# A fused memory attention and bilinear FFN on one Trainium2 core: the quarters of M formed on VectorE straight out of PSUM, low parts on GpSimd

## The chip, the core and the metric

The kernel runs on one core of one Trainium2 chip. The metric is the device time of one execution in microseconds (us); it was measured in three runs of the kernel before, and one more execution was taken with the profiler, whose trace the prediction reads.

## What is computed

There are 8 batches with 8 heads, 576 positions and head size 64; phi has 32 memory slots. Attention goes through the slots, and its output feeds a bilinear feed-forward net. Cut to what matters:

```python
a = softmax(phi, over positions)                  # per batch and head
k_m, v_m = a^T k, a^T v                           # 32 x 64 memories per head
attn = softmax(q k_m^T / 8, over the 32 slots)
x = attn v_m                                      # 4608 tokens x 512
h = (x w1) * (x w2)                               # 4608 x 1024
out = (h w3) w_out                                # 4608 x 512, fp32
```

## The kernel before

The kernel folds matrices together so that TensorE does less. W = w3 w_out is formed once, at the start. For each batch, v_m is multiplied into w1 and w2, which gives the batch's matrix **M**; attention probabilities **P** times M give the two factors of h directly. All large products run as three float32r products of split operands: a high part (a cast, made on ScalarE) and a low part (the value less its high part), called h and l in names: mh and ml for M, ahl for P, gh and gl for the product of the factors, Wh and Wl for W.

From batch 1 on, P times M is done as a 2 by 2 block product with seven block products instead of eight (class `Sevenths`), so besides the blocks themselves P and M need four sums of blocks each; the seven blocks and sums lie in one tile of 7 slices. `sums` makes the four sums of P on GpSimd (line 364) and the parts of all seven. `memory_weights` makes a quarter of M (M0 to M3, 256 columns of each block): it multiplies v_m with the staged weights (`weights_times`, line 385) into the two PSUM banks `a` and `b`, copies both banks to a tile x on ScalarE (line 423), makes the four sums on GpSimd (line 426), casts on ScalarE (line 133) and subtracts on VectorE (line 135), first for the three blocks, then for the four sums. The tile x has one buffer, so a quarter can't be copied out before the quarter ahead of it is through.

A batch b has two stages. In the **product stage** (`ab_stage`) TensorE does the 8 groups of seven products of batch b (line 661), pair by pair; ScalarE and VectorE combine banks `a`, `b` and `o` (lines 680 to 726), and GpSimd makes gl (line 729). In the **output stage** (`out_stage`) TensorE multiplies gh, gl with W (line 765) in blocks of 128 rows, 24 matmuls each, four blocks for an even batch and five for an odd one; ScalarE copies each block out of its PSUM bank `o`, of which there are two, to `osb` (line 775), and SP stores it. Under the output stage of batch b the attention of batch b+1 and its M run as well: scores (`sc`, line 310), their softmax in two halves (`se`, `sn`, `pr`, lines 320 to 349), `ps` (the step `sums`), and M0 to M3.

Every engine works through its instructions in the order in which the program was written; a scheduler does not move them. That order comes from hand-written strings: REST is the order of one output stage (O is a quarter of an output block, six matmuls, and with the block's last quarter its copy to osb; M0, se0 and the like go one step further in their generator; W0 to W3 start the load of a quarter's weights, and phi2, rows2, q2, kv2 start loads for batch b+2). MEETS places the steps that run inside a product stage, by pair, with a "<" for a step left over from the output stage before. One quarter O always stays for the product stage, after its first two products (q1 into bank `a`, q5 into bank `o`).

```python
REST = """
W0 W1 O blocks blocks O sc0 sc1 sc0 W2 se0 se0 sc1 O O M0 W3 M0 se0 se1 se1 M0 se1 M1 sn0 sn0 sn0 pr0 M0 M0 O
M1 M0 sn1 sn1 sn1 pr1 O M1 M1 ps M2 O ps O M1 M1 M2 O phi2 rows2 ps ps M2 M2 M3 O q2 kv2 M2 M2 O M3 O M3 M3
""".split()
```

The functions that the change touches, and what calls them:

Of the kernel before, what the change touches and what calls it, by code (L numbers as in the profile page):

```python
# [8 lines left out]
F32 = mybir.dt.float32  # L9
F32R = mybir.dt.float32r  # L10
# [4 lines left out]
ALU = mybir.AluOpType  # L15
# [25 lines left out]
B15 A15 A14 less.1 A15 A15 B14 A15 B2 A13 less.1 A2 A14 A2 A14 A13 A2 A14 less.1 B13 A14 A12 A13 A13 less.1 B12 A13  # L41
A12 mem.1 A12 A12 A12 mem.1
""".split()
MEETS = {0: "<M3 top", 1: "<M3 exp", 2: "top exp", 3: "row", 4: "norm", 6: "less less", 7: "less less less"}
REST = """
W0 W1 O blocks blocks O sc0 sc1 sc0 W2 se0 se0 sc1 O O M0 W3 M0 se0 se1 se1 M0 se1 M1 sn0 sn0 sn0 pr0 M0 M0 O
M1 M0 sn1 sn1 sn1 pr1 O M1 M1 ps M2 O ps O M1 M1 M2 O phi2 rows2 ps ps M2 M2 M3 O q2 kv2 M2 M2 O M3 O M3 M3
""".split()


# [1 line left out]
def memory_attention__then__bilinear_ffn_kernel(  # L52
# [19 lines left out]
    nc = tc.nc  # L72
    P = 128
    B, NG, S = qT.shape[0], 4, 576
    D = 64
    M = 32
    NT = 2
# [8 lines left out]
    const = ctx.enter_context(tc.tile_pool(name="const", bufs=1))  # L86
# [13 lines left out]
    NQ = 4  # L100
    FQ = DF // NQ
# [9 lines left out]
    for x, where in (("h", Wh), ("l", Wl)):  # L111
        t = const.tile([P, half, DO], F32R, name=f"W{x}0")
# [12 lines left out]
    def banks_ab():  # L125

        return [psum(ps_ab, x) for x in "ab"]
# [4 lines left out]
    def split(hi, lo, src):  # L132
        nc.scalar.copy(out=hi, in_=src)  # L133
        yield
        nc.vector.tensor_tensor(out=lo, in0=src, in1=hi.bitcast(F32), op=ALU.subtract)  # L135
# [50 lines left out]
    ready = {}  # L186

    def attention(b):
# [167 lines left out]
        def sums():  # L356
            x = v["at"].rearrange("p n (t s) -> p (n t) s", t=NT)
            hi, lo = ready["P", b] = [att.tile([P, 7, HALF], F32R, name="ahl", tag="ahl", bufs=2) for _ in range(2)]
            s = att.tile([P, 4, HALF], F32, name="sums", tag="a")

            for y, i, j, op in ((0, 3, 2, ALU.add), (1, None, 0, ALU.subtract), (2, 0, 3, ALU.subtract), (3, 1, 1, ALU.subtract)):
                p = s[:, y - 1] if i is None else x[:, i]
                q = s[:, 1] if y == 3 else x[:, j]
                nc.gpsimd.tensor_tensor(out=s[:, y], in0=p, in1=q, op=op)  # L364
            yield from split(hi[:, :3], lo[:, :3], x[:, :3])
            yield
            yield from split(hi[:, 3:], lo[:, 3:], s)

        steps = {"ps": sums, "top": top, "row": row, "less": less, "exp": exp, "norm": norm, "mem": memories, "blocks": blocks}
        steps |= {f"turn{i}": lambda i=i: turn(i) for i in (0, 4)}  # L370
        for n in range(2):
# [9 lines left out]
    def weights_times(b, q, w, ps):  # L381
        for g in range(NG):
            for t in range(NT):
                d = slice((1 - t) * D, (2 - t) * D)
                nc.tensor.matmul(
                    ps[t][g * M : (g + 1) * M], lhsT=vm[b % 2][d, g], rhs=w[d, :, g], start=True, stop=True
                )
# [19 lines left out]
    staged = {}  # L407
# [9 lines left out]
    def memory_weights(b, q):  # L417
        ps = banks_ab()
        weights_times(b, q, staged[q], ps)
        yield  # L420
        x = const.tile([P, 8, FQ], F32, name="x", tag=f"w12_{NQ - 1}")
        for t in range(NT):
            nc.scalar.copy(out=x[:, 2 * t : 2 * t + 2], in_=ps[t].rearrange("p (w f) -> p w f", w=2))  # L423
        yield
        for y, i, j in ((4, 0, 1), (6, 3, 0), (5, 3, 4), (7, 2, 5)):
            nc.gpsimd.tensor_tensor(out=x[:, y], in0=x[:, i], in1=x[:, j], op=ALU.subtract)  # L426
        mh, ml = ready["M", b][q] = [new.tile([P, 7, FQ], F32R, name=f"{z}{q}") for z in ("mh", "ml")]
        yield from split(mh[:, :3], ml[:, :3], x[:, 1:4])
        yield
        yield from split(mh[:, 3:], ml[:, 3:], x[:, 4:])  # L430


    tasks, at = [], 0
# [4 lines left out]
    CW = DF  # L438
# [292 lines left out]
    def ab_stage(b, go, before, part):  # L731
# [4 lines left out]
        for p in range(NF + 2):  # L736
            for x in order:
                if x == "+":
                    for what in MEETS.get(p, "").split():
                        if what[0] == "<":  # L740
# [48 lines left out]
    new = ctx.enter_context(tc.tile_pool(name="new", bufs=1, side="right", reuse_waits="tile"))  # L789

    def goer(b):
        begun = {}

        def go(what):
            if b + 1 == B:
                return
            if what not in begun:
                if what[0] == "M":
                    begun[what] = memory_weights(b + 1, int(what[1]))
                else:  # L800
                    begun[what] = steps[b + 1][what]()
            next(begun[what], None)

        return go
# [108 lines left out]
```

## Time and profile before

| | us |
|---|---|
| median of three runs | 579.94 (577.59 to 580.29) |
| the profiled execution's own time | 579.34 |
| its span, first to last instruction | 577.6 |
| TensorE (PE) busy, 91% of the span | 528.4 |
| VectorE (DVE) busy | 374.7 |
| ScalarE (ACT) busy | 315.9 |
| GpSimd (POOL) busy | 217.7 |

The profile calls TensorE's matmuls PE and its weight loads PEld. A busy share is an average over stages with different limits, so the table alone doesn't say what a change is worth. A matmul counts as busy at either clock, so busy time also holds the price of a low clock. In rows of the trace, out<-in gives the names of the tiles, then partitions x elements, and x with a number is how many instructions a row holds.

### The profile page before, as it was taken

How to read it: one execution, taken by the hardware profiler on the slowest of the kernel's cores; microseconds unless marked ns; L12 is line 12 of the kernel's file. 1: busy time of each engine (PE TensorE's matmuls, PEld its weight loads, DVE VectorE, ACT ScalarE, POOL GpSimd, SP SyncE). 2: the span in 40 equal slices, each digit the busy share in tenths (PEclk: the TensorE clock that was granted, in tenths of full speed). 3: DMA queues.
4: the chain of work that ended last, by engine and by line, in shares of the span. 5: the costliest groups of instructions: out<-in, count | busy, mean ns of one | idle time of the engine just before them, and what ended most of it. 6: DMA issues, size and time to landing. Idle time of an engine off the chain costs nothing.

```text
span 577.6 us, 10059 instructions
## 1 busy us (share of the span) xinstructions
PE 528.4 (91%) x3879; PEld 420.2 (73%) x3879; DVE 374.7 (65%) x643; ACT 315.9 (55%) x574; POOL 217.7 (38%) x203
## 2 busy tenths in 40 slices
PE   8999999977999699978999699968999699969997
PEld 5457698656966499657967498648967498548987
DVE  4899997675758466866757366865767366865500
ACT  7998785355635365356635365446545365446501
POOL 0000000283436524383447424383437424374500
PEclk9999999995999899997999799997999799998999
DMA  8999569827064601772075502671084512600011
GB/s 343 421 416 420 211 238 362 311 76 306 11 237 172 285 28 52 259 273 110 10 272 189 231 29 81 231 309 73 11 295 185 213 28 93 220 18 37 1 37 54
DMA packets 21823, 103.28 MB, mean 179 GB/s; under 512 B 2576, under 2 KB 3728, under 8 KB 12816
## 3 DMA queue, kind: packets, MB, share of 16 engines
q1 hardware_dynamic: 21776, 102.65, 46.3%
q8 instruction: 30, 0.49, 0.3%
q14 instruction: 17, 0.14, 0.1%
HBM read 89.00 MB, written 13.64 MB: 178 GB/s over the span
## 4 chain that ended last, share of the span: by engine, by line
PE 63%; POOL 16%; DVE 11%; ACT 6%; issue 2%; DMA 1%; SPq 0%; ACTq 0%; DVEq 0%
PE o L765 17%; PE b L661 13%; POOL x L426 10%; PE o L661 8%; PE a L661 8%; POOL sums L364 6%; DVE ml L135 4%; PE a L547 3%; ACT x L423 3%; PE b L547 3%; PE x L267 3%; PE o L547 2%; DVE s_sb L341 1%; ACT mh L133 1%; DMA raw<-in_weights 1%
## 5 line engine op out<-in xcount | busy, mean ns | idle before, releaser
L426 POOL TENSOR_TENSOR x<-x 128x256 f32<-128x256 f32 x112 | 104.0, 951 | 138.1 <-ACT x L423 135.9
L729 POOL TENSOR_TENSOR gl<-u,gh 128x576 fp32r<-128x576 f32 x56 | 79.7, 1428 | 136.4 <-ACT gh L726 134.7
L765 PE MATMUL o<-W,gh 128*128 128x512 f32 (+1 forms) x296 | 102.1, 402 | 0.0
L135 DVE TENSOR_TENSOR ml<-x,mh 128x1024 fp32r<-128x1024 f32 (+1 forms) x60 | 75.6, 1270 | 34.5 <-ACT mh L133 34.5
L661 PE MATMUL b<-ahl,mh 128*128 128x288 f32 x336 | 75.6, 308 | 3.5 <-ACT b L680 3.2
L765 PE MATMUL o<-Wh,gh 128*128 128x512 f32 (+1 forms) x148 | 62.2, 420 | 16.7 <-ACT osb L775 16.7
L133 ACT CAST mh<-x 128x1024 fp32r<-128x1024 f32 (+1 forms) x60 | 56.9, 948 | 29.8 <-POOL x L426 29.3
L765 PEld LDWEIGHTS o<-W,gh 128*128 128x128 f32 x296 | 57.5, 196 | 20.2 <-issue 8.9
L661 PE MATMUL o<-ahl,mh 128*128 128x288 f32 x224 | 50.8, 308 | 22.3 <-ACT osb L775 19.5
L661 PEld LDWEIGHTS b<-ahl,mh 128*128 128x128 f32 x336 | 54.9, 192 | 8.0 <-ACT b L680 4.0
L765 PE MATMUL o<-Wh,gl 128*128 128x512 f32 (+1 forms) x148 | 59.2, 400 | 0.0
L775 ACT COPY osb<-o 128x512 f32<-128x512 f32 (+1 forms) x37 | 21.4, 579 | 68.9 <-PE o L765 68.9
L765 PE MATMUL o<-Wl,gh 128*128 128x512 f32 (+1 forms) x148 | 59.0, 399 | 0.0
L765 PE MATMUL o<-W,gl 128*128 128x512 f32 (+1 forms) x148 | 58.6, 396 | 0.0
L765 PEld LDWEIGHTS o<-Wh,gh 128*128 128x128 f32 x148 | 29.2, 197 | 35.0 <-ACT osb L775 17.9
L661 PEld LDWEIGHTS o<-ahl,mh 128*128 128x128 f32 x224 | 37.5, 196 | 23.6 <-ACT osb L775 20.2
L661 PE MATMUL b<-ahl,ml 128*128 128x288 f32 x168 | 50.4, 300 | 0.0
L661 PE MATMUL a<-ahl,mh 128*128 128x288 f32 x224 | 49.6, 304 | 0.8 <-ACT x L423 0.8
L680 ACT COPY b<-a 128x288 f32<-128x288 f32 x56 | 21.7, 388 | 39.1 <-DVE u L719 19.9
L703 DVE TENSOR_TENSOR o<-b,a_sb 128x288 f32<-128x288 f32 x56 | 25.8, 460 | 25.2 <-PE b L661 24.9
L423 ACT COPY x<-a 128x512 f32<-128x512 f32 x28 | 16.4, 587 | 46.2 <-DVE ml L135 37.1
L661 PEld LDWEIGHTS a<-ahl,mh 128*128 128x128 f32 x224 | 38.0, 197 | 1.8 <-ACT x L423 1.3
(156 smaller groups left out, 1096.3 us busy)
## 6 DMA issues: line engine op xcount, KB each, us to landing
kv<-kept SPq DMA_DIRECT2D x21, 1024.0 KB
kv<-in_kv SPq DMA_DIRECT2D x16, 1024.0 KB, 11.4
raw<-in_weights SPq DMA_DIRECT2D x10, 1024.0 KB, 18.6
q<-in_qT SPq DMA_DIRECT2D x8, 1152.0 KB
out<-osb SPq DMA_DIRECT2D x31, 256.0 KB, 2.0
q<-kept SPq DMA_DIRECT2D x7, 1024.0 KB, 5.4
raw<-in_weights SPq DMA_DIRECT2D x12, 512.0 KB, 4.1
ph<-in_phiT SPq DMA_DIRECT2D x9, 576.0 KB, 4.0
```

The source lines that it names most:

```text
L133: nc.scalar.copy(out=hi, in_=src)
L135: nc.vector.tensor_tensor(out=lo, in0=src, in1=hi.bitcast(F32), op=ALU.subtract)
L364: nc.gpsimd.tensor_tensor(out=s[:, y], in0=p, in1=q, op=op)
L423: nc.scalar.copy(out=x[:, 2 * t : 2 * t + 2], in_=ps[t].rearrange("p (w f) -> p w f", w=2))
L426: nc.gpsimd.tensor_tensor(out=x[:, y], in0=x[:, i], in1=x[:, j], op=ALU.subtract)
L547: nc.tensor.matmul(pw[r][i], lhsT=x[:, i * P : (i + 1) * P], rhs=y, start=k == 0 and j == 0, stop=k == NF - 1 and j == len(pairs) - 1,)
L661: nc.tensor.matmul(ps, lhsT=x[:, j], rhs=y[:, i], start=start and k == 0, stop=stop and k == 2, skip_group_check=True,)
L680: nc.scalar.copy(out=self.u, in_=self.a)
L703: nc.vector.tensor_tensor(out=self.c, in0=self.u, in1=self.s5, op=ALU.add)
L729: nc.gpsimd.tensor_tensor(out=self.cut(gl), in0=self.gr, in1=self.cut(gh).bitcast(F32), op=ALU.subtract)
L765: nc.tensor.matmul(ps, lhsT=x[f][:, at : at + P], rhs=y[f][:, cols], start=f == 0 and k == 0, stop=f == NF - 1 and k == 2,)
L775: nc.scalar.copy(out=osb[:, cols], in_=ps)
```

## The change

It rewrites how a quarter of M and the parts of P are made, and moves steps in the two strings.

- `memory_weights`: ScalarE copies only one block (t4, 256 columns) to x, and casts the other three straight from PSUM to mh. VectorE makes the four sums, one operand from PSUM each, in an order that builds them one on another, and subtracts the low parts of the three blocks, again out of PSUM. ScalarE then casts the four sums in one piece, and GpSimd subtracts their low parts in two pieces. A quarter has four steps instead of six.
- The tile x holds two quarters' sums, used by M0 and M3 and by M1, and M2 takes a buffer of the tile `u`, which the product stage uses for gr: three buffers in place of one.
- `sums`: GpSimd subtracts both low parts of P, which VectorE did.
- REST and MEETS: both exponentials go ahead of M0's copies, phi2 and rows2 go ahead of q2, M1's product comes one O later, M3's last steps come earlier, and inside the product stage top, exp, row, norm and less come one pair earlier.

```diff
-MEETS = {0: "<M3 top", 1: "<M3 exp", 2: "top exp", 3: "row", 4: "norm", 6: "less less", 7: "less less less"}
+MEETS = {0: "<M3 top", 1: "top exp", 2: "exp row", 3: "norm", 5: "less less", 6: "less less", 7: "less"}
 REST = """
...
+W0 W1 O blocks blocks O sc0 sc1 sc0 W2 se0 se0 sc1 se0 O se1 se1 se1 O M0 W3 phi2 rows2 sn0 sn0 sn0 pr0 M0 M0 O M1 M0 M1
+sn1 sn1 sn1 pr1 O O ps M1 M2 q2 M2 O ps M1 O M2 O M3 kv2 M3 M2 O M3 M3
...
-            yield from split(hi[:, :3], lo[:, :3], x[:, :3])
-            yield
-            yield from split(hi[:, 3:], lo[:, 3:], s)
+            for i, j, y in ((0, 3, x[:, :3]), (3, 7, s)):
+                nc.scalar.copy(out=hi[:, i:j], in_=y)
+                nc.gpsimd.tensor_tensor(out=lo[:, i:j], in0=y, in1=hi[:, i:j].bitcast(F32), op=ALU.subtract)
+                yield
...
-        yield
-        x = const.tile([P, 8, FQ], F32, name="x", tag=f"w12_{NQ - 1}")
-        for t in range(NT):
-            nc.scalar.copy(out=x[:, 2 * t : 2 * t + 2], in_=ps[t].rearrange("p (w f) -> p w f", w=2))
-        yield
-        for y, i, j in ((4, 0, 1), (6, 3, 0), (5, 3, 4), (7, 2, 5)):
-            nc.gpsimd.tensor_tensor(out=x[:, y], in0=x[:, i], in1=x[:, j], op=ALU.subtract)
+        (b12, b11), (b21, b22) = [[x[:, k * FQ : (k + 1) * FQ] for k in range(2)] for x in ps]
+        yield
+        if "x" not in staged:
+            staged["x"] = const.tile([P, 2, 4, FQ], F32, name="x", tag=f"w12_{NQ - 1}")
+        if q == 2:
+            x = const.tile([P, CW], F32, name="u", bufs=2).rearrange("p (k f) -> p k f", k=4)
+        else:
+            x = staged["x"][:, int(q == 1)]
+        t1, t2, t3, t4 = [x[:, k] for k in range(4)]
         mh, ml = ready["M", b][q] = [new.tile([P, 7, FQ], F32R, name=f"{z}{q}") for z in ("mh", "ml")]
-        yield from split(mh[:, :3], ml[:, :3], x[:, 1:4])
-        yield
-        yield from split(mh[:, 3:], ml[:, 3:], x[:, 4:])
+        firsts = ((0, 1, b11), (1, 3, ps[1].rearrange("p (k f) -> p k f", k=2)))
+        nc.scalar.copy(out=t4, in_=b12)
+        for i, j, y in firsts:
+            nc.scalar.copy(out=mh[:, i:j], in_=y)
+        yield
+        for y, p, r in ((t1, t4, b11), (t3, b22, t4), (t2, b22, t1), (t4, b21, t2)):
+            nc.vector.tensor_tensor(out=y, in0=p, in1=r, op=ALU.subtract)
+        for i, j, y in firsts:
+            nc.vector.tensor_tensor(out=ml[:, i:j], in0=y, in1=mh[:, i:j].bitcast(F32), op=ALU.subtract)
+        yield
+        nc.scalar.copy(out=mh[:, 3:], in_=x)
+        for k in range(0, 4, 2):
+            y = slice(3 + k, 5 + k)
+            nc.gpsimd.tensor_tensor(out=ml[:, y], in0=x[:, k : k + 2], in1=mh[:, y].bitcast(F32), op=ALU.subtract)
```

Two places show how the order moves. The first is ScalarE at the end of the output stage of batch 2, from the cast of P's four sums on. In it mh_2640 and mh_2692 of the kernel before are M2 and M3, mh_2578, mh_2628 and mh_2682 after the change are M1, M2 and M3, and the last osb but one is the copy of the third output block. Before:

```order
L133 CAST ahl<-sums 128x1152
L133 CAST mh_2640<-x 128x768
L133 CAST mh_2640<-x 128x1024
L423 COPY x<-a 128x512
L423 COPY x<-b 128x512
L775 COPY osb<-o 128x512
L133 CAST mh_2692<-x 128x768
L680 COPY b<-a 128x288
L684 COPY a_sb<-o 128x288
L775 COPY osb<-o 128x512
L133 CAST mh_2692<-x 128x1024
```

With the change:

```order
L366 CAST ahl<-sums 128x1152
L441 CAST mh_2578<-x 128x1024
L432 COPY x<-a 128x256
L434 CAST mh_2682<-a 128x256
L434 CAST mh_2682<-b 128x512
L441 CAST mh_2628<-u 128x1024
L441 CAST mh_2682<-x 128x1024
L789 COPY osb<-o 128x512
L694 COPY b<-a 128x288
L698 COPY a_sb<-o 128x288
L789 COPY osb<-o 128x512
```

The copy of the third block still stands behind M3; now M3's last cast is ahead of it as well, and what these casts wait for is VectorE and no longer GpSimd.

The second place is GpSimd in the same output stage, from M0 up to the first gl of the product stage. Before (line 426 are the sums of a quarter of M, line 364 those of P):

```order
L426 TENSOR_TENSOR x<-x 128x256 x8
L364 TENSOR_TENSOR sums<-at 128x288
L364 TENSOR_TENSOR sums<-sums,at 128x288
L364 TENSOR_TENSOR sums<-at 128x288
L364 TENSOR_TENSOR sums<-at,sums 128x288
L426 TENSOR_TENSOR x<-x 128x256 x8
L729 TENSOR_TENSOR gl_622<-u,gh_614 128x576
```

With the change:

```order
L444 TENSOR_TENSOR ml_2548<-x,mh_2547 128x512 x2
L364 TENSOR_TENSOR sums<-at 128x288
L364 TENSOR_TENSOR sums<-sums,at 128x288
L364 TENSOR_TENSOR sums<-at 128x288
L364 TENSOR_TENSOR sums<-at,sums 128x288
L367 TENSOR_TENSOR ahl<-at,ahl 128x864
L367 TENSOR_TENSOR ahl<-sums,ahl 128x1152
L444 TENSOR_TENSOR ml_2579<-x,mh_2578 128x512 x2
L444 TENSOR_TENSOR ml_2629<-u,mh_2628 128x512 x2
L444 TENSOR_TENSOR ml_2683<-x,mh_2682 128x512 x2
L743 TENSOR_TENSOR gl_622<-u,gh_614 128x576
```

Ahead of P's sums there is now one quarter of M instead of two; behind them come P's two low parts and then M1, M2 and M3, all of them ahead of the first gl.

## Rows read from the trace of the kernel before

**Rows 1.** What TensorE waited for: us in total, times, longest us

```profile
PE o L661 <- ACT osb L775: 19.5, 3, 6.5
PE o L765 <- ACT osb L775: 16.7, 3, 5.6
PE b L661 <- ACT b L680: 3.2, 1, 3.2
PE o L661 <- ACT ahl L133: 2.0, 1, 2.0
PE a L661 <- ACT x L423: 0.8, 1, 0.8
PE o L661 <- DVE ahl L135: 0.8, 1, 0.8
```

**Rows 2.** Stretches around seven transitions: length, PE busy, granted clock, DMA share, GB/s

```profile
128.00:141.00 13.00, 8.76 (x29) 0.50 0.97 380
196.00:200.00 4.00, 3.33 (x8) 0.57 0.42 161
261.00:268.50 7.50, 5.82 (x21) 0.54 0.37 145
322.00:330.00 8.00, 5.14 (x13) 0.57 0.46 183
387.00:398.00 11.00, 6.38 (x23) 0.53 0.51 207
452.00:460.00 8.00, 5.87 (x16) 0.57 0.38 151
517.00:524.50 7.50, 3.42 (x11) 0.54 0.09 35
```

**Rows 3.** Chain that ended last, from 236 to 264: start, us, what

```profile
239.00 0.76 DVE small L336
...
241.64 0.78 DVE at L349
...
254.06 3.20 POOL x L426 x3
...
258.67 1.05 ACT mh L133
...
262.14 0.50 ACT osb L775
...
262.68 1.09 PE o L661 x3
```

**Rows 4.** Timeline of PE and DVE, output stage of batch 2: start, us

```profile
236.13 0.61 PE L385 MATMUL a<-kv,vm 64*32 64x512 f32 x1
...
236.88 0.76 DVE L329 TENSOR_TENSOR s_sb<-s_sb,small 128x576 f32<-128x576 f32 x1
...
238.01 0.50 PE L765 MATMUL o<-Wh,gh 128*128 128x512 f32 x1
...
255.88 0.29 PE L661 MATMUL a<-ahl,ml 128*128 128x288 f32 x1
```

**Rows 5.** VectorE by line; min/median/max ns where three numbers stand

```profile
L703 DVE TENSOR_TENSOR o<-b,a_sb 128x288 f32<-128x288 f32 x56 | 25.8, 460 | 25.2 <-PE b L661 24.9
...
L341 DVE TENSOR_TENSOR s_sb<-s_sb,small x16: 745/901/1065, 58.4 to 504.0; 128x576 f32<-128x576 f32 x16
...
L338 DVE TENSOR_SCALAR small<-small x16: 174/176/415, 57.4 to 503.5; 128x18 f32<-128x18 f32 x16
```

**Rows 6.** ScalarE, a copy of 256 columns out of PSUM: busy us, mean ns

```profile
L775 ACT COPY osb<-o 128x256 f32<-128x256 f32 x2 | 0.7, 373 | 4.8 <-PE o L765 4.8
```

**Rows 7.** GpSimd by line: min/median/max ns, first and last start

```profile
L729 POOL TENSOR_TENSOR gl<-u,gh x56: 1417/1429/1440, 145.2 to 548.2; 128x576 fp32r<-128x576 f32 x56
...
L364 POOL TENSOR_TENSOR sums<-at x14: 801/1215/1627, 122.1 to 510.9; 128x288 f32<-128x288 f32 x14
```

**Rows 8.** DMA issues: a staged quarter of weights, KB, median us to landing

```profile
q<-kept SPq DMA_DIRECT2D x7, 1024.0 KB, 5.4
```

More of the change, by code (lines that the diff above doesn't have):

```diff
@@ L43 @@
 """.split()
-MEETS = {0: "<M3 top", 1: "<M3 exp", 2: "top exp", 3: "row", 4: "norm", 6: "less less", 7: "less less less"}
+MEETS = {0: "<M3 top", 1: "top exp", 2: "exp row", 3: "norm", 5: "less less", 6: "less less", 7: "less"}
 REST = """
-W0 W1 O blocks blocks O sc0 sc1 sc0 W2 se0 se0 sc1 O O M0 W3 M0 se0 se1 se1 M0 se1 M1 sn0 sn0 sn0 pr0 M0 M0 O
-M1 M0 sn1 sn1 sn1 pr1 O M1 M1 ps M2 O ps O M1 M1 M2 O phi2 rows2 ps ps M2 M2 M3 O q2 kv2 M2 M2 O M3 O M3 M3
+W0 W1 O blocks blocks O sc0 sc1 sc0 W2 se0 se0 sc1 se0 O se1 se1 se1 O M0 W3 phi2 rows2 sn0 sn0 sn0 pr0 M0 M0 O M1 M0 M1
+sn1 sn1 sn1 pr1 O O ps M1 M2 q2 M2 O ps M1 O M2 O M3 kv2 M3 M2 O M3 M3
 """.split()
@@ L419, in memory_weights @@
         weights_times(b, q, staged[q], ps)
+        (b12, b11), (b21, b22) = [[x[:, k * FQ : (k + 1) * FQ] for k in range(2)] for x in ps]
         yield
-        x = const.tile([P, 8, FQ], F32, name="x", tag=f"w12_{NQ - 1}")
-        for t in range(NT):
-            nc.scalar.copy(out=x[:, 2 * t : 2 * t + 2], in_=ps[t].rearrange("p (w f) -> p w f", w=2))
+        if "x" not in staged:
[5 more added lines that the diff above has]
+        t1, t2, t3, t4 = [x[:, k] for k in range(4)]
+        mh, ml = ready["M", b][q] = [new.tile([P, 7, FQ], F32R, name=f"{z}{q}") for z in ("mh", "ml")]
+        firsts = ((0, 1, b11), (1, 3, ps[1].rearrange("p (k f) -> p k f", k=2)))
+        nc.scalar.copy(out=t4, in_=b12)
+        for i, j, y in firsts:
+            nc.scalar.copy(out=mh[:, i:j], in_=y)
         yield
-        for y, i, j in ((4, 0, 1), (6, 3, 0), (5, 3, 4), (7, 2, 5)):
-            nc.gpsimd.tensor_tensor(out=x[:, y], in0=x[:, i], in1=x[:, j], op=ALU.subtract)
-        mh, ml = ready["M", b][q] = [new.tile([P, 7, FQ], F32R, name=f"{z}{q}") for z in ("mh", "ml")]
-        yield from split(mh[:, :3], ml[:, :3], x[:, 1:4])
+        for y, p, r in ((t1, t4, b11), (t3, b22, t4), (t2, b22, t1), (t4, b21, t2)):
+            nc.vector.tensor_tensor(out=y, in0=p, in1=r, op=ALU.subtract)
+        for i, j, y in firsts:
+            nc.vector.tensor_tensor(out=ml[:, i:j], in0=y, in1=mh[:, i:j].bitcast(F32), op=ALU.subtract)
         yield
-        yield from split(mh[:, 3:], ml[:, 3:], x[:, 4:])
+        nc.scalar.copy(out=mh[:, 3:], in_=x)
+        for k in range(0, 4, 2):
+            y = slice(3 + k, 5 + k)
+            nc.gpsimd.tensor_tensor(out=ml[:, y], in0=x[:, k : k + 2], in1=mh[:, y].bitcast(F32), op=ALU.subtract)
     tasks, at = [], 0
```

## The prediction

> **What bounds the kernel now.** I first read the waits of TensorE, since it is busy in most of the span. [rows 1] show that its idle time has almost one cause: six waits of 5.6 and 6.5 us for an osb copy on ScalarE, three in front of an output block and three in front of q5, and four smaller ones in the first transition. They add up to 19.5 + 16.7 + 3.2 + 2.0 + 0.8 + 0.8 = 43.0 us, all at the end of seven output stages. The windows around these waits come next: [rows 2] show the granted clock at 0.50 to 0.57 there, so TensorE also works at 1.2 instead of 2.4 GHz for a while after each wait; it fell after TensorE had stood still. In these seven windows it was busy for 38.7 us. The stretches at full clock in them are at most the sum of (2 x clock - 1) x length, 4.7 us, so between 34.0 and 38.7 us of work ran at half clock, which would take half as long at full clock: a loss of 17.0 to 19.4 us. I take 17.0. Everything around the transitions is dense, so TensorE is the bound and the waits are what can be won.
>
> Why it waits, the chain tells [rows 3]: GpSimd's sums for M2 end at 257.3 and the last of them at 258.7, ScalarE then casts them, VectorE makes the low part, which frees x; only then can ScalarE copy M3 out, and the osb copy at 262.14 is written behind those copies. The output block itself was ready: TensorE had worked through the next one as well and finished its last product before the wait at 256.17 [rows 4]. So the copy is held by its queue alone, and q5 starts at 262.68 because it needs that bank.
>
> **What is removed.** x is no longer one buffer and M's sums leave GpSimd, so the chain of copy, GpSimd, cast, VectorE, copy is gone in each quarter. If nothing replaced it, 43.0 + 17.0 us would go.
>
> **What is added, on one ruler.** I lay out the output stage of batch 2, from M0 at 236.13 on.
>
> TensorE: M0 and M1 together take 238.01 - 236.13 = 1.88, so 0.94 each [rows 4]. From 236.13 to 256.17 it did four of these, eleven quarters of output blocks and q1 (0.55, the last two rows of its work), so a quarter with its switching takes (20.04 - 3.76 - 0.55) / 11 = 1.43. With the change M0, a quarter, M1 and two quarters end at 242.30. Then M2 needs the banks of M0, and these are now free when VectorE's six operations on M0 are over, not when ScalarE has copied them. That is a new wait.
>
> VectorE: its last score step ends at 237.64 [rows 4]. The half softmax up to `at` took 3.42 there, from 239.00 to 242.42 [rows 3], with one instruction at 1.07 that takes 0.745 undisturbed and one at 0.42 that takes 0.176 [rows 5]; GpSimd is now idle beside it, so 2.86. The exponential it waits for now stands ahead of osb and M0 on ScalarE. So `at` is done at 240.50. The trace has no VectorE operation of 256 columns with one operand in PSUM, but 288 take 0.460 [rows 5] and 576 with both in SBUF 0.76 [rows 4], a slope of 1.04 ns a column: 0.43 for 256, 0.69 for 512. M0's six are 5 x 0.43 + 0.69 = 2.84 and end at 243.34. TensorE waits **1.04 us** in front of M2. M2 and three quarters then end at 248.57. VectorE's second half softmax runs beside GpSimd's low parts of M0 and takes 3.02, M1's six 2.84: 249.20. TensorE waits **0.63 us** in front of M3, which ends at 250.14; five quarters and q1 end at 257.84, where q5 comes.
>
> The Trainium skill ("VectorE: DVE Perf Modes", section Rules for kernel authors) advises for elementwise work on a matmul's output either to accept the plain rate from PSUM or to copy to SBUF first where many operations follow, which speaks against this edit with its six. If reading PSUM cost half the rate, the six would take 4.7 us and the two waits would grow by 3.7 us a stage, 26 us in all, to 559. The rows just used show the same slope from either memory, so the sum goes without it.
>
> GpSimd: M0's sums are done at 242.22, ScalarE's cast of 1024 columns (1.05, [rows 3]) at 243.27. From 288 columns in 0.80 and 576 in 1.43 [rows 7] a column costs 2.2 ns: the two pieces of M0 take 2.6, P's four sums 3.2, its low parts of 864 and 1152 columns 2.06 and 2.69. With `at` ready at 246.36, P is complete at 254.3, 3.5 us ahead of q5. The bound from above is P's sums at 1.63 [rows 7], when VectorE works beside them, and it becomes a rival below. The work that VectorE does beside P's parts reads one operand from PSUM, and gl never took over 1.44 us [rows 7] beside such operations; I take the lower value.
>
> ScalarE: P's second cast ends at about 250.8, M1's at 251.8, M3's copies (0.37 + 0.37 + 0.59, [rows 6] and the osb copy) at 253.1, M2's cast at 254.2; VectorE's sums of M3 follow the copy and end at 254.9, so M3's cast ends at 255.9 and the osb copy behind it at 256.5, 1.3 us ahead of q5. Where the next thing is late, it is this copy. In odd stages there are four quarters more in front of q5, and the copies are further ahead.
>
> SP and the loads: the store of the first block moves behind both exponentials, to about 239, and W3 queues behind it; 1024 KB take 5.4 us to land [rows 8], so 245, and M3 needs it at 249.2. phi2 and rows2 go behind W3. The moves inside the product stage keep three pairs between row and less. I cost all this at nothing; the cover is 4 us.
>
> The first transition has three quarters fewer in front of q5: on this ruler TensorE is there at 253.55, P's low part at 254.3 and ScalarE's copy of bank a about 0.6 behind TensorE's need, 1.35 us more.
>
> **Sum**, against the profiled execution's own 579.34: - 43.0 - 17.0 + 7 x (1.04 + 0.63) + 1.35 + 0.7 (an extra switch of 0.1 a stage) = **533 us**. That execution lies 0.6 below the median of the runs, which changes nothing. The new waits are a fifth of the old ones in length and come after long full work, so I expect the clock to stay full.
>
> **Rivals.**
> 1. *VectorE holds the banks longer.* The six operations lie on one another, and an operation disturbed by GpSimd went from 0.745 to 1.065 [rows 5], a factor of 1.43. At that price they take 4.06; the waits become 2.26 and 1.84, 2.43 us a stage more: 550. For it: nothing hides them now. Against: no row with a PSUM operand is stretched. 14%.
> 2. *The old queue stays.* The osb copy still stands behind M3. If VectorE or ScalarE is 3 us later there than laid out, q5 of the even stages waits 2 us, and the clock may fall again: 533 + 3 x 2 + up to 3 x 2 = 545. That would be the change not doing what it says, in part. 5%.
> 3. *GpSimd becomes the bound.* With everything at the disturbed rate, M0 ends at 248.5, P's sums at 255.0 and its low parts at 264.5. Even stages then wait 6.7 us, and about 2.4 for the clock, odd ones 0.9, the first 11 and 4.4: about 45 us back, 578, no change. For it: P's low parts, 4.7 us, have moved onto the chain. 7%. The Trainium skill ("SBUF — State Buffer", section Who interferes with whom) says that a VectorE tensor_tensor contends with GpSimd's reads where both its inputs are in SBUF. By that rule the new VectorE work, with an input in PSUM, leaves GpSimd alone; the undisturbed gl agrees, and the chance stays low for it.
> 4. *Slower than before: gl queues behind M's low parts.* M1, M2 and M3 follow P on GpSimd and all stand ahead of the first gl; `u` has two buffers, so the third pair's gr waits for the first gl. It decides once M3's low parts end later than some 9 us after q1, about 266: in the layout they end at 262.2, at the disturbed rate at 280. Then every stage pays some 11 us on top of rival 3: 578 + 77 = 655. It needs all of GpSimd's work disturbed. 3%.
>
> **Chances and range.** The forecast gets 70%; its own range is 523 to 543: below, the waits in front of M2 and M3 vanish and the half-clock loss is 19.4 (517 at the extreme); above, they double. Rivals 1 and 2 reach to 550; 1% is left for anything else. Rivals 3 and 4 are left out of the range, which runs from 523 to 552 and leaves some 17% outside. A difference under 0.5%, 2.9 us, can't be told from none here. Faster by more than that: 93% (the forecast, rivals 1 and 2, the odd 1%, and the 3% of rival 3 that come out below 576); within it: 4%, the rest of rival 3; slower: 3%, rival 4.
>
> **What would show it.** Right: the waits of TensorE for osb are gone or under 1 us each; new waits of about 1 us in front of M2 and 0.6 in front of M3, for VectorE, seven of each; granted clock 1.00 through the transitions from 196 on; P's low parts on GpSimd at about 2.1 and 2.7 us; six VectorE operations of a quarter in 2.8 us; the first gl no later behind q1 than now. Wrong: a clock row at 0.5 in an even stage (rivals 2 or 3, told apart by whether ScalarE or GpSimd released q5), VectorE operations of 256 columns over 0.5 us (rival 1), VectorE waiting for gl in the product stage (rival 4).

## The result, and the profile after

The changed kernel takes **529.88 us** (median of four executions, 528.88 to 531.52) against 580.12 for the kernel before on the same chip: a ratio of 0.914, 95% interval 0.910 to 0.918. The profiled execution took 529.76, with a span of 528.0. The forecast was 533, the range 523 to 552.

The waits of TensorE in the changed kernel (us in total, times, longest us) answer to [rows 1]:

```profile
PE a L386 <- ACT mh L434: 3.5, 7, 0.5
...
PE o L675 <- POOL ahl L367: 0.9, 1, 0.9
```

No line with osb is left. What is left in the transitions is a wait in front of a quarter of M (L386), once in each, and in the first transition 0.9 for P's low part.

The stretches around three of the seven transitions, each from M0 to past q5 (length, PE busy, PEld, DVE, ACT, POOL busy, granted clock, DMA share, GB/s), answer to [rows 2]:

```profile
109.00:129.00 20.00, 18.60 (x123) 11.16 (x122) 17.64 (x37) 11.53 (x22) 11.23 (x9) 1.00 0.72 264
161.00:183.00 22.00, 21.52 (x134) 13.69 (x133) 18.60 (x38) 12.54 (x23) 13.18 (x11) 1.00 0.83 310
221.00:244.00 23.00, 22.48 (x141) 14.61 (x140) 18.81 (x39) 13.36 (x25) 13.98 (x11) 1.00 0.82 315
```

The clock is at 2.4 GHz throughout; in [rows 2] it was at 0.50 to 0.57 behind each wait.

VectorE in the output stage of batch 2, from M0's six operations to M3's (start, busy us; several at a time are merged):

```profile
225.70 0.38 DVE L437 TENSOR_TENSOR x<-x,a 128x256 f32<-128x256 f32 x1
...
227.46 0.68 DVE L439 TENSOR_TENSOR ml<-b,mh 128x512 fp32r<-128x512 f32 x1
228.06 0.74 DVE L336 TENSOR_REDUCE small<-s_sb 128x18 f32<-128x576 f32 x1
228.83 0.85 DVE L338 TENSOR_SCALAR small<-small 128x18 f32<-128x18 f32 x1
...
230.01 1.50 DVE L341 TENSOR_TENSOR s_sb<-s_sb,small 128x576 f32<-128x576 f32 x1
231.55 0.78 DVE L349 STREAM_TRANSPOSE at<-s_sb 128x576 f32<-128x576 f32 x1
...
234.01 0.68 DVE L439 TENSOR_TENSOR ml<-b,mh 128x512 fp32r<-128x512 f32 x1
```

GpSimd and TensorE in the same stage:

```profile
228.37 2.53 POOL L444 TENSOR_TENSOR ml<-x,mh 128x512 fp32r<-128x512 f32 x2 [10.30 <-ACT mh L441]
232.47 0.81 POOL L364 TENSOR_TENSOR sums<-at 128x288 f32<-128x288 f32 x1 [1.57 <-DVE at L349]
...
237.65 2.70 POOL L367 TENSOR_TENSOR ahl<-sums,ahl 128x1152 fp32r<-128x1152 f32 x1
```

```profile
227.75 0.39 PE L779 MATMUL o<-W,gh 128*128 128x512 f32 x1
...
229.30 0.50 PE L779 MATMUL o<-W,gh 128*128 128x512 f32 x1
...
233.29 0.39 PE L779 MATMUL o<-Wl,gh 128*128 128x512 f32 x1
234.19 1.01 PE L386 MATMUL a<-kv,vm 64*32 64x512 f32 x2 [0.52 <-ACT mh L434]
...
235.86 0.50 PE L779 MATMUL o<-W,gh 128*128 128x512 f32 x1
...
243.06 0.29 PE L675 MATMUL a<-ahl,ml 128*128 128x288 f32 x1
243.19 0.42 PE L675 MATMUL o<-ahl,mh 128*128 128x288 f32 x2
```

ScalarE's copy of the third block, which q5 needs:

```profile
241.15 0.58 ACT L789 COPY osb<-o 128x512 f32<-128x512 f32 x1
```

M0's six operations run from 225.70 to 228.14, 2.44 us. Then comes the second half softmax, 4.27 us from 228.06 to 232.33, with L338 at 0.85 and L341 at 1.50; both start while GpSimd works off the low parts of M0 (228.37 to 230.90). M1's six end at 234.69, so M3 on TensorE starts at 234.19 with its bank a and at 234.84 with bank b. The last product of the quarter ahead of it started at 233.29. Where nothing is waited for, M follows 0.33 behind such a product and lasts 1.02 until the next one (M0 in this stage); here the next one started at 235.86, so M3 waited 235.86 - 233.29 - 1.35 = 1.22. M2, with 227.75 and 229.30, waited 0.2. Read so, all seven stages show 0.20 to 0.21 for M2 and 1.17 to 1.22 for M3. The list names ScalarE's cast for this wait; M1's cast had long ended, and VectorE's reading of bank a ended at 234.09.

### The profile page after: what moved, and what is told of

The parts are those of the page before. It is cut to its first block, busy times and chain, and to the rows that moved or that the text cites. A ratio compares the mean times of both kernels' runs of the same rounds, so it can differ in the third digit from the quotient of the medians.

```text
span 528.0 us, 10212 instructions
## 1 busy us (share of the span) xinstructions
PE 516.9 (98%) x3879; PEld 407.2 (77%) x3879; DVE 360.9 (68%) x741; ACT 295.4 (56%) x574; POOL 205.4 (39%) x161
## 4 chain that ended last, share of the span: by engine, by line
PE 65%; DVE 22%; DMA 5%; issue 4%; ACT 2%; POOL 1%; SPq 0%; ACTq 0%; DVEq 0%
PE o L779 22%; PE b L675 13%; PE o L675 8%; PE a L675 8%; DMA kv<-in_weights 4%; DVE s_sb L341 3%; PE x L267 3%; DVE s_sb L320 2%; DVE small L327 2%; DVE s_sb L329 2%; PE a L561 2%; DVE x L437 2%; PE b L561 2%; DVE small L336 2%; DVE small L338 1%
## 5 line engine op out<-in xcount | busy, mean ns | idle before, releaser
L444 POOL TENSOR_TENSOR ml<-x,mh 128x512 fp32r<-128x512 f32 x42 | 53.5, 1295 | 120.2 <-ACT mh L441 120.2
L779 PEld LDWEIGHTS o<-W,gh 128*128 128x128 f32 x296 | 55.1, 188 | 25.1 <-issue 14.7
L675 PE MATMUL b<-ahl,mh 128*128 128x288 f32 x336 | 73.5, 301 | 0.2 <-DVE gr L725 0.2
L779 PE MATMUL o<-Wh,gh 128*128 128x512 f32 (+1 forms) x148 | 59.2, 400 | 0.0
L779 PE MATMUL o<-Wl,gh 128*128 128x512 f32 (+1 forms) x148 | 57.1, 386 | 0.0
L779 PE MATMUL o<-Wh,gl 128*128 128x512 f32 (+1 forms) x148 | 56.9, 384 | 0.0
L675 PE MATMUL b<-ahl,ml 128*128 128x288 f32 x168 | 49.6, 295 | 0.0
L675 PE MATMUL o<-ahl,mh 128*128 128x288 f32 x224 | 48.3, 296 | 0.9 <-POOL ahl L367 0.9
L733 DVE TENSOR_TENSOR u<-b,gr 128x288 f32<-128x288 f32 x56 | 25.6, 458 | 24.6 <-PE b L675 24.4
L725 DVE TENSOR_TENSOR gr<-b,a_sb 128x288 f32<-128x288 f32 x56 | 25.4, 454 | 22.8 <-PE b L675 22.1
L740 ACT CAST gh<-u 128x576 fp32r<-128x576 f32 x56 | 37.4, 679 | 1.6 <-DVE u L733 1.6
```

Of the source, the lines that this page charges most:

```text
L444: nc.gpsimd.tensor_tensor(out=ml[:, y], in0=x[:, k : k + 2], in1=mh[:, y].bitcast(F32), op=ALU.subtract)
L675: nc.tensor.matmul(ps, lhsT=x[:, j], rhs=y[:, i], start=start and k == 0, stop=stop and k == 2, skip_group_check=True,)
L725: nc.vector.tensor_tensor(out=self.c22, in0=self.u, in1=self.s5, op=ALU.add)
L733: nc.vector.tensor_tensor(out=self.gr[:, 1], in0=self.u, in1=self.c22, op=ALU.mult)
L740: nc.scalar.copy(out=self.cut(gh), in_=self.gr)
L779: nc.tensor.matmul(ps, lhsT=x[f][:, at : at + P], rhs=y[f][:, cols], start=f == 0 and k == 0, stop=f == NF - 1 and k == 2,)
```

## The experiments

Ten kernels. A time without a range is of one execution; the kernel before had medians of 579.1 to 579.7 beside them.

### Which part carries the gain

**The new order alone.** The kernel before, with the order strings of the change (each of its steps of M and P mapped, so that with one x every quarter's last step stands ahead of the next quarter's copy):

```diff
-W0 W1 O blocks blocks O sc0 sc1 sc0 W2 se0 se0 sc1 O O M0 W3 M0 se0 se1 se1 M0 se1 M1 sn0 ...
+W0 W1 O blocks blocks O sc0 sc1 sc0 W2 se0 se0 sc1 se0 O se1 se1 se1 O M0 W3 phi2 rows2 sn0 ...
```

> The kernel before with the new order alone: exponentials ahead of M0, the loads and the osb copies moved, the product stage's steps moved; sums of M still on GpSimd out of one x, low parts of P still on VectorE. Theory A (the one x buffer ties ScalarE's queue, and the osb copy in it, to GpSimd's chain of sums): the chain of four quarters is as long as before, so TensorE still waits for osb, 35 to 50 us in all, with the half clock behind the waits, and the time is 565 to 590. Theory C (the order brings the gain, since the exponentials no longer stand behind osb and M0): the osb waits fall below 15 us and the time is 545 or less.

641.86: neither. It is 62 us slower than before. The waits:

```profile
PE o L765 <- ACT osb L775: 43.7, 3, 14.6
PE o L661 <- ACT osb L775: 32.8, 3, 10.9
PE a L661 <- ACT x L423: 19.7, 4, 8.0
```

They are of the same kind as in [rows 1], and together more than twice as long (96.2 against 43.0). In batch 2 the osb copy starts 35.3 us behind M0 (254.28 to 289.62), where before it was 25.9 (236.13 to 262.02). Of these 9.4 us, 1.4 come from M0's copies, which now stand behind both exponentials, so that GpSimd's sums begin later. Another 4.3 come from the place of the osb copy itself: before, it stood right behind M3's copies, and now it stands behind M3's last cast, which waits for M3's sums:

```profile
288.67 1.04 ACT L133 CAST mh<-x 128x1024 fp32r<-128x1024 f32 x1 [2.40 <-POOL x L426]
289.62 0.58 ACT L775 COPY osb<-o 128x512 f32<-128x512 f32 x1
```

In the rest of the way P's four sums stand ahead of M1's on GpSimd; what that alone costs was not taken apart. So theory A holds for what is waited for, and its size was wrong: for the old chain the new order is the worse one.

**One x with the new engines.** The kernel after, VectorE's sums and all, with one buffer:

```diff
-        if q == 2:
-            x = const.tile([P, CW], F32, name="u", bufs=2).rearrange("p (k f) -> p k f", k=4)
-        else:
-            x = staged["x"][:, int(q == 1)]
+        x = staged["x"][:, 0]
```

> The kernel after with all quarters in one x buffer and the steps of M1, M2 and M3 put so that each quarter's last step stands ahead of the next quarter's copy; VectorE's sums out of PSUM and P's low parts on GpSimd stay. Theory A: M2's copy on ScalarE has to wait for M1's low parts, which stand behind P's low parts on GpSimd (242.9 on the clock of batch 2, M0 at 221.5), M3's copy for M2's low parts (249.4), M3's cast ends at 253.5 and osb behind it at 254, 11 us behind TensorE's need at 243.2: osb waits of 11 us in even stages, 5 us in odd ones, with half clock behind them: 530 + 3 x 11 + 4 x 5 + about 20 = 590 to 605. Theory B (VectorE's faster sums bring the gain, buffers only a little): waits under 2 us a stage, 530 to 545.

612.86. The waits:

```profile
PE o L779 <- ACT osb L789: 26.2, 3, 8.8
PE o L675 <- ACT osb L789: 19.5, 3, 6.6
PE a L675 <- DVE ml L439: 15.2, 4, 6.7
```

Theory A, a little above its 590 to 605. M2's copy stands idle on ScalarE until GpSimd has done M1's low parts:

```profile
266.92 0.37 ACT L432 COPY x<-a 128x256 f32<-128x256 f32 x1 [5.05 <-POOL ml L444]
```

**Two x buffers.** The same lines, with two in turn and no use of `u`:

```diff
+        x = staged["x"][:, q % 2]
```

> The kernel after with two x buffers in turn (M0 and M2 in one, M1 and M3 in the other) and nothing else changed. Theory A: only M3's copy is held, by M1's low parts behind P's on GpSimd (242.9 on the clock of batch 2); M3's sums end at 246, its cast at 247, osb at 247.6, 4.4 us behind TensorE's need at 243.2 in the even stages, in time in the odd ones, which have four quarters (5.7 us) more in front of q5: 530 + 3 x 4.4 + up to 3 x 4 for the clock = 543 to 556, waits for osb in three stages alone. Theory B: as after, 530 within 3.

564.8, where theory A allowed up to 556. The waits are 10.8 and 7.9 for osb and 4.4 in the first transition; they come in all six later transitions and not in three, since osb is needed by an output block too (2.6 us each) where q5 is far. The third buffer is worth 35 us, of which 10.8 + 7.9 + 4.4 = 23.1 are waits. The other 11.8 are put down to the lower clock behind them: its mean is 0.978 here and 1.00 in the kernel after, which can cost up to 0.022 x 563 = 12.4.

**The old order with the new code.** The order strings of before, on the kernel after (M0's six ahead of the softmax, M2 and M3 with two quarters between them):

```diff
-... se0 O se1 se1 se1 O M0 W3 phi2 rows2 sn0 sn0 sn0 pr0 M0 M0 O M1 ...
+... O O M0 W3 M0 se0 se1 se1 M0 se1 M1 sn0 sn0 sn0 pr0 M0 O M1 ...
```

> The kernel after with the order strings of before (M's and P's steps mapped onto their new, fewer steps): M0's six operations ahead of the softmax on VectorE, the exponentials behind M0's copies, the loads for the next batch late again, top, exp and row in their old places in the product stage. Theory A (the buffers and VectorE's sums carry the gain, the new order little): 526 to 536. Theory C (the new order is needed for it, because the exponentials behind M0's copies make P late): P's low parts release q5 in even stages, waits of 3 us or more there, 540 or more.

556.53 (554.58 to 558.56), ratio to before 0.961 (0.957 to 0.964). The number is theory C's, the mechanism is not: P does not release q5. TensorE waits in front of M3:

```profile
PE a L386 <- ACT ahl L366: 18.8, 6, 3.1
PE a L386 <- DVE ml L439: 2.7, 1, 2.7
```

```profile
241.63 0.42 DVE L439 TENSOR_TENSOR ml<-a,mh 128x256 fp32r<-128x256 f32 x1
...
242.15 1.03 PE L386 MATMUL a<-kv,vm 64*32 64x512 f32 x1 [3.13 <-ACT ahl L366]
```

```profile
242.00:246.00 4.00, 3.85 (x19) 1.56 (x20) 0.64 (x2) 2.37 (x3) 4.00 (x5) 0.50 0.00 0
246.00:248.00 2.00, 2.00 (x6) 1.52 (x6) 1.14 (x3) 1.25 (x4) 2.00 (x1) 0.50 0.86 254
248.00:250.00 2.00, 2.00 (x10) 1.63 (x9) 1.39 (x4) 1.47 (x3) 2.00 (x3) 0.89 1.04 385
```

M3 needs the banks of M1, and M1's six stand behind both half softmaxes on VectorE; VectorE's last reading of bank a (L439) ends at 242.05, 0.1 ahead of M3. The old order gives TensorE too little other work until then. The windows show what a wait of 3.13 costs on top: the clock stands at half for some 6 us behind it.

**The buffers with the old engines.** ScalarE's raw copies go into two buffers in turn, GpSimd's sums into two more, and all low parts of M and P are on VectorE, each step as early as the buffers let it.

```diff
+        r = staged["x"][:, q % 2]
+        x = const.tile([P, CW], F32, name="u", bufs=2).rearrange("p (k f) -> p k f", k=4)
...
-            nc.vector.tensor_tensor(out=y, in0=p, in1=r, op=ALU.subtract)
+            nc.gpsimd.tensor_tensor(out=y, in0=p, in1=s, op=ALU.subtract)
```

> The buffers without the change of engines: ScalarE's raw copies into two buffers in turn, GpSimd's sums into two more, all low parts of M and of P on VectorE, as in the kernel before; the new order with each quarter's steps as early as the buffers let them. GpSimd has four quarters at 3.0 to 4.0 and P's sums at 3.2 to 6.4 one behind the other, from 226.5 on the clock of batch 2: M3's sums end at 242 to 249, its cast 1 later, osb behind it at 243.7 to 250.7, where TensorE needs it at 242. Theory A (what counts is that the copies no longer wait for GpSimd's chain): 1.7 to 5 us in three stages with half clock behind the longer ones, 530 to 550. Theory B (the sums must leave GpSimd): waits for osb as before or nearly, in six stages, 560 to 580.

593.54 (592.92 to 595.23), ratio 1.025 (1.022 to 1.028): slower than before, beyond theory B. GpSimd works without a gap for long, and its operations stand beside VectorE's low parts. P's sums, which take 0.80 in the kernel after:

```profile
250.88 1.70 POOL L364 TENSOR_TENSOR sums<-at 128x288 f32<-128x288 f32 x1 [0.29 <-DVE at L349]
252.65 1.51 POOL L364 TENSOR_TENSOR sums<-sums,at 128x288 f32<-128x288 f32 x1
```

M3's sums end 27.6 behind M0's start here (239.56 to 267.19). That is not later than before, where it was 29.1 (236.13 to 265.24). But the osb copy stands behind M3's last cast in the new order, and so it starts 28.6 behind M0, where before it was 25.9:

```profile
267.23 1.04 ACT L437 CAST mh<-u 128x1024 fp32r<-128x1024 f32 x1 [2.92 <-POOL u L434]
268.18 0.58 ACT L785 COPY osb<-o 128x512 f32<-128x512 f32 x1
```

By these numbers it is that place of the copy that makes this kernel slower than before. It is not shown by a run: the same buffers with the copy left ahead of M3's casts were not tried.

Buffers, engines and order are not three shares of a sum. Against the whole change, the two others without the order lose 27 us, without the engines 64, without the buffers 83, and the order alone 112.

### VectorE's sums out of PSUM or out of a raw copy

**Sums on VectorE out of a raw copy.** Three result buffers, VectorE's sums and GpSimd's work as in the change, but with ScalarE's raw copy in between:

```diff
+        for t in range(NT):
+            nc.scalar.copy(out=r[:, 2 * t : 2 * t + 2], in_=ps[t].rearrange("p (w f) -> p w f", w=2))
...
-        for y, p, r in ((t1, t4, b11), (t3, b22, t4), (t2, b22, t1), (t4, b21, t2)):
+        for y, p, s in ((t1, b12, b11), (t3, b22, b12), (t2, b22, t1), (t4, b21, t2)):
```

> The kernel after, but ScalarE first copies each quarter out of PSUM into one raw buffer, as the kernel before did and as the Trainium skill advises where many operations follow (VectorE: DVE Perf Modes, Rules for kernel authors), and VectorE's sums and first low part read SBUF alone; results in x, u, u, x; order and GpSimd's work as in the change. Theory D (VectorE's reading of the banks makes the waits in front of M2 and M3): ScalarE's copy frees them at about 226.5 and 229 on the clock of batch 2, so both waits go, 7 x 1.5 = 10 us, against it P's sums on GpSimd, which now stand beside VectorE operations with both operands in SBUF: at 1.6 instead of 0.8 each, as where that happened in the kernel before, P is complete at 243.5, where TensorE needs it at 241.7: 1.8 us back in even stages, 3 in the first: 529.9 - 10 + 3 x 1.8 + 3 = 528, within 523 to 534. If GpSimd is not touched: 520. Rival (the copies through SBUF cost more than they free, since M2's raw copy waits in ScalarE's queue for VectorE's six on M1, and osb behind it): 535 to 545.

589.31 (587.79 to 591.41), ratio 1.018 (1.014 to 1.022). All three numbers of the expectation were far too low. Theory D had the waits right: read as above, nothing is waited for in front of M2 and M3 in any stage. What it had mis-sized is what came back. VectorE on M0 and M3 of one stage, and GpSimd beside M3:

```profile
242.37 1.51 DVE L437 TENSOR_TENSOR x<-x 128x256 f32<-128x256 f32 x4
243.80 0.95 DVE L438 TENSOR_TENSOR ml<-x,mh 128x768 fp32r<-128x768 f32 x1
...
258.80 6.07 DVE L437 TENSOR_TENSOR x<-x 128x256 f32<-128x256 f32 x4 [1.00 <-ACT x L433]
264.79 2.02 DVE L438 TENSOR_TENSOR ml<-x,mh 128x768 fp32r<-128x768 f32 x1
```

```profile
260.29 5.71 POOL L443 TENSOR_TENSOR ml<-u,mh 128x512 fp32r<-128x512 f32 x4
266.02 3.17 POOL L443 TENSOR_TENSOR ml<-x,mh 128x512 fp32r<-128x512 f32 x2
```

On M0, with GpSimd idle, the work takes 2.38 us, as much as out of PSUM (2.44). On M3, beside GpSimd's low parts, the same work takes 8.01, and GpSimd's pieces go from 1.29 to 1.43 and 1.58 each. M1 to M3 together take 16.1 instead of 7.6, and waits for the one raw buffer add 0.78 + 1.00. P's sums on GpSimd, expected at 1.6 each, took 0.83 to 1.00: VectorE paid the larger part. M3's cast and the osb copy behind it come that much later, and the osb waits are back (24.8 + 15.2). Two raw buffers were not tried, so a part of the loss belongs to the single one.

The prediction set the Trainium skill's advice for a matmul's output, to accept the plain rate from PSUM or to copy to SBUF first where many operations follow ("VectorE: DVE Perf Modes", section Rules for kernel authors), against the slopes in [rows 4, 5]. The run decides: the copy fails here, and not because of the reading rate (2.38 against 2.44).

The Trainium skill ("SBUF — State Buffer", section Who interferes with whom) says that a VectorE operation with two inputs in SBUF contends with a GpSimd operation that reads SBUF, and that one with at most one input there doesn't, outside the modes in which VectorE uses both of its ports. The sums and low parts of this run and of the kernel after agree: 256 columns out of SBUF alone took 0.38 us with GpSimd idle and up to 1.83 beside it, and with one operand in PSUM never more than 0.43. L338 has one input, in SBUF, and was held all the same (0.85 instead of 0.18), so it could only fall under that exception; no run here shows the mode it ran in.

### What TensorE still waits for

**The low parts out of PSUM done twice**, 1.09 us more of VectorE in each quarter:

```diff
-        for i, j, y in firsts:
+        for i, j, y in firsts * 2:
             nc.vector.tensor_tensor(out=ml[:, i:j], in0=y, in1=mh[:, i:j].bitcast(F32), op=ALU.subtract)
```

> The kernel after with the two low parts out of PSUM on VectorE done twice, 0.41 + 0.68 = 1.09 us more in each quarter. Theory D (VectorE's six operations hold M0's and M1's banks, so the prediction's waits are theirs): M2's wait grows from 0.25 to 1.35, M3's from 1.25 by 2.18 - 1.10 to 2.33, 7 x 2.18 = 15 us: 543 to 549, and the list of waits names VectorE's ml in front of M2 or M3. Theory E (ScalarE's casts release M3, as the list names them): VectorE has that much slack, 529 to 533.

539.02, 9.1 us more: theory D's direction, theory E is out, and the size is below D's 13 to 19. The list names ScalarE's copies in front of M2 and M3 and not VectorE's ml, as D had expected. Read in the way shown above, M2 waits 1.13 in batch 2 (1.35 expected) and M3 1.72 (2.33 expected). For M3 a part fell away: the second half softmax had moved against GpSimd's pieces, so that only L338 met one, and it took 3.85 instead of 4.27:

```profile
231.64 1.16 DVE L338 TENSOR_SCALAR small<-small 128x18 f32<-128x18 f32 x1
...
233.14 0.76 DVE L341 TENSOR_TENSOR s_sb<-s_sb,small 128x576 f32<-128x576 f32 x1
```

**M0's low parts behind P's sums** on GpSimd, by a step boundary behind P's sums:

```diff
-... pr0 M0 M0 O M1 M0 M1 sn1 sn1 sn1 pr1 O O ps M1 M2 ...
+... pr0 M0 M0 O M1 M1 sn1 sn1 sn1 pr1 O O ps M0 ps M1 M2 ...
```

> The kernel after with one thing moved: the low parts of M0 on GpSimd stand behind P's sums, no longer beside VectorE's second half softmax; VectorE's and TensorE's order stay as in the change. Theory D (GpSimd's pieces beside it stretch that half softmax from 2.77, as it took in the run with the softmax first, to 4.27): it takes 2.8, M1's six end 1.4 earlier and the wait in front of M3 (1.25) goes; M2's 0.25 stays. P is complete later by M0's low parts less the 1.4, some 1.2 us, which leaves 0.4 us ahead of q5 in even stages and adds some 2.4 in the first transition: 529.9 - 7 x 1.25 + 2.4 = 523.5, within 521.5 to 526. Theory E (the stretch is VectorE's own, not GpSimd's): L338 and L341 stay at 0.85 and 1.50 there, M3's wait stays: 530 to 535.

526.36 (524.63 to 528.57), ratio 0.907 (0.905 to 0.910). Of theory D the mechanism is shown. All sixteen L338 and L341 (min/median/max ns) are undisturbed, and TensorE's wait in front of M3 is gone:

```profile
L338 DVE TENSOR_SCALAR small<-small x16: 176/177/177, 56.7 to 458.9; 128x18 f32<-128x18 f32 x16
...
L341 DVE TENSOR_TENSOR s_sb<-s_sb,small x16: 745/759/759, 57.6 to 459.4; 128x576 f32<-128x576 f32 x16
```

The median is just above what was expected, and the first transition is where it goes: it waits for P's low parts 1.1 and 1.9, where 0.9 stood. These 2.1 us more are less than the 2.4 that were expected, but the clock stands at half behind them, which the expectation had not counted:

```profile
132.00:134.00 2.00, 2.00 (x7) 1.61 (x7) 0.00 (x0) 0.40 (x1) 2.00 (x3) 0.50 0.99 418
```

From M0 of this transition to M0 of the next it is 55.77 us instead of 51.98. The profiled execution, 528.57, is the slowest of the four; its first M0 already starts 2.3 later than in the kernel after (111.57 against 109.30).

**Both half softmaxes first.** VectorE does them ahead of M0's six, P's sums stand ahead of M0's low parts on GpSimd, and two quarters of output blocks move to the place between M1 and M2.

```diff
-... pr0 M0 M0 O M1 M0 M1 sn1 sn1 sn1 pr1 O O ps M1 M2 q2 M2 O ps M1 O M2 O M3 ...
+... pr0 M0 O M1 M1 sn1 sn1 sn1 pr1 M0 O O ps M0 ps M1 O O M2 q2 M2 ps M1 O M3 ...
```

> The kernel after with both halves of the softmax ahead of M0's six operations on VectorE, P's sums ahead of M0's low parts on GpSimd, and two quarters of output blocks moved from between M2 and M3 to between M1 and M2. Theory D (TensorE's waits in front of M2 and M3, 0.25 and 1.25 us, come from VectorE, whose second half softmax was stretched from 2.9 to 4.27 us by GpSimd's low parts of M0 beside it): with GpSimd idle beside both halves they take 2.9 each, at is complete 4 us earlier, M0's six end at 230.3 on the clock of batch 2 and M1's at 232.8, where TensorE is at 230.5 and 232.9: the waits go, 7 x 1.5 to 1.8 us: 517 to 521, ratio to after 0.977 to 0.983. Theory E (those 1.5 us are switching and issue of TensorE, or ScalarE's casts as the list of waits names them): no change, 528 to 531; the wait in front of M3, named for ScalarE, stays at 0.5.

**521.45** (520.58 to 521.60), ratio to before 0.899 (0.897 to 0.901): 8.4 us less than the change, and the fastest of all. The second half softmax takes 2.77 us (223.23 to 226.00), no wait for a quarter of M is listed (read as above, the 1.2 in front of M3 is gone in all stages and 0.24 in front of M2 is left), and from M0's start to the end of q1 it is 20.66 (219.02 to 239.68) instead of 21.86. 7 x 1.20 = 8.4, the whole gain. The 1.5 to 1.8 a stage that theory D expected counted in M2's wait, which stayed: the time is 0.4 above its range.

**P's low parts on VectorE again**, the first behind M1's six and the second behind M2's:

```diff
-                nc.gpsimd.tensor_tensor(out=lo[:, i:j], in0=y, in1=hi[:, i:j].bitcast(F32), op=ALU.subtract)
+                nc.vector.tensor_tensor(out=lo[:, i:j], in0=y, in1=hi[:, i:j].bitcast(F32), op=ALU.subtract)
```

> The kernel after with P's low parts on VectorE again, the first behind M1's six operations, the second behind M2's. Theory F (moving them to GpSimd took about 2.5 us off VectorE's path to M3's cast and the osb copy behind it): M2's six end at 238.5 on the clock of batch 2, the second low part at 240.2, M3's six at 242.7, the cast at 243.7 and osb at 244.3, 1.1 us behind TensorE's need: waits for osb of about 1 us in three stages, 531 to 537. Theory G (their place is indifferent, since VectorE and GpSimd both have room): 528 to 531. If VectorE's operations are stretched by GpSimd beside them, up to 545.

537.83 (537.45 to 537.97), ratio 0.928 (0.927 to 0.930): theory F, 0.8 above its range. The waits for osb are the expected 1.1 in three stages; 3.0 in the first transition, where 0.9 stood, had not been counted. With 0.6 in front of output blocks they make 6.1 of the 8.0; the rest has no row of its own:

```profile
PE o L675 <- ACT osb L789: 3.4, 3, 1.2
PE a L675 <- DVE ml L439: 2.1, 1, 2.1
...
PE b L675 <- ACT b L694: 0.9, 1, 0.9
```

So moving P's low parts is worth 8 us, although GpSimd takes 4.7 us for what costs VectorE 2.6.

## Why the prediction came out right

**The waits: right.** All of 43.0 us [rows 1] went. The osb copy ends at 241.73 in batch 2, 1.46 ahead of q5 (1.3 was laid out). The experiments with one and two x buffers show the chain named in the prediction: ScalarE's copies held by x, and osb in their queue.

**The clock: right, undersized.** The loss of 17.0 was taken from bounds of 17.0 to 19.4. By the result, 579.34 - 529.76 = 49.6 less 43.0, plus what came back (7 x 1.82 + 0.9), leaves 20.2. The term's own working shows where the rest was lost: in [rows 2] all of the low clock was caught (the windows' lengths times 1 - clock add up to 27.2, the span times 1 - 0.953 to 27.1), so the choice of the lower bound, which took every stretch at full clock for work, was the mistake. The upper bound, 19.4, would have given 530.7. The 0.8 beyond it stays open. The 1.82 is not the reason: all three even stages show the same 21.86 against 20.04, and the odd ones 27.3, just four quarters of an output block more.

**The new waits: right in sum by luck, wrong in place.** 1.04 in front of M2, 0.63 in front of M3 and 0.1 of switching, 1.77 a stage, were predicted; 1.82 came (21.86 against 20.04 from M0's start to the end of q1). But M2 waits about 0.2, M3 about 1.2, and some 0.4 are left for switching and issue. Three steps failed, and their errors happened to cancel. Switching was laid out at 0.1, and TensorE needs M2 0.4 later than laid out. The six operations were laid out one behind the other, 2.84; they overlap a little and take 2.44. Their sizes, 0.43 and 0.69, were about right (0.38 to 0.43 and 0.68), but the slope behind them was drawn through one row with an operand in PSUM and one out of SBUF, so it couldn't show that both memories have the same slope; the raw copy does (2.38 against 2.44). And the second half softmax was given 3.02 beside GpSimd's low parts, 0.16 over the first half, although [rows 5] had shown L338 and L341 stretched; it took 4.27. The two runs that keep GpSimd away from it show the cause: it falls back to 2.77, and the 1.2 in front of M3 goes.

**P on GpSimd: right.** The low parts took 2.06 and 2.70, P's sums 0.80, gl stayed at 1.43; P is complete at 240.35, 2.84 ahead of q5 (3.5 was laid out; the longer softmax took the difference). In the first transition 0.9 was waited, 1.35 predicted.

**The rivals.** Rival 1, a stretch of the operations on PSUM, did not come: L437 and L439 of 256 columns took 0.38 to 0.43 in every case. Its mechanism is real for operations that read SBUF alone, as the raw copy shows, and there by more than the factor of 1.43 that it was priced at. Rival 2, osb still too late, was 1.46 us away; with two x buffers it is what happens. Rivals 3 and 4 were ruled out by the rows of GpSimd: nothing there ran at the disturbed rate, and M3's low parts end at 247.85 in batch 2, 3.5 us ahead of the first gl.

## What to carry to other kernels

Before an operation moves between VectorE and GpSimd, ask of each operation beside it whether it reads SBUF alone or has an operand in PSUM: here the same sums on the same engine made 530 us out of PSUM and 589 out of one raw buffer in SBUF. A tiny operation can be held too (L338). When a queue is freed by more buffers, ask at once which engine holds the next resource, and give TensorE other work until then: here the new order alone lost 62 us, buffers and engines without it gained 23, and all three together 50. Ask as well what stands ahead of the copy that everything waits for. A small operation that is held in a profile was best priced here by the piece beside it, not by a factor.

## What the runs showed of the hardware

An operation as small as L338, 128 x 18, took 0.84 to 1.17 us beside GpSimd's low parts instead of 0.18. It ended where a piece of GpSimd's ended: at 229.68 in the kernel after, where two pieces of 1.29 (the median of L444) lie between 228.37 and 230.90, and in the run with the low parts twice at 232.80, where GpSimd's second piece ended at 232.77. In all seven stages of both runs the two ends lie within 0.04 us. So it cost the rest of the piece, whatever its own length. L238 of the product stage, 128 x 2 and 0.16 alone, did the same beside gl in the kernel after: 0.92 to 1.22, ending within 0.03 of gl's end in six stages. The reciprocal behind L338 (L339) lies wholly beside a piece of GpSimd's and took its usual 0.27.

The reading of PSUM cost VectorE next to nothing: 0.38 to 0.43 for 256 columns with one operand there, and the six operations of a quarter 2.44 against 2.38 for the same work out of SBUF.

The clock stayed at 1.00 in the transitions of the change with a wait of about 1.2 us in each, and stood at 0.50 behind waits of 3.1 with the old order. Between the two, the same wait did either. With two x buffers, TensorE waited 2.62 us for osb up to 193.53 and again up to 318.49; the clock fell behind the first and not behind the second:

```profile
194.00:196.00 2.00, 2.00 (x7) 1.52 (x6) 0.00 (x0) 0.00 (x0) 2.00 (x3) 0.50 0.68 262
318.00:320.00 2.00, 1.51 (x7) 1.25 (x8) 0.46 (x1) 0.93 (x2) 2.00 (x2) 1.00 0.35 136
```

By the times, the lower clock cost some 11.8 us for waits of 23.1 in all (two x buffers), and about 20 for 43 (the kernel before), a little under 3 us a transition in the latter.
